# Drains behind conv bursts, later Gram matmuls, and narrower second-phase loads in a ConvNeXt-V2 block kernel

## The chip, the cores and the metric

The kernel runs on one core of one Trainium2 chip. The metric is the device time of a run in microseconds (us), best read as the median of several runs. Every run quoted here was in the fast state, with a granted TensorE clock of 0.988 to 0.998. Profiled executions are 1.7 to 1.9 us shorter by their span than by their time, so spans are compared with spans and times with times.

## The reference, cut to what matters

```python
# x: [1, 512, 512, 96] bf16
out = depthwise_conv3x3(x, dw)                 # zero padding
h = layernorm(out)                             # over the 96 channels
h = gelu(h @ w1)                               # 96 -> 384
gx = sqrt((h * h).sum(over all pixels) + 1e-6) # one number per expanded channel
nx = gx / (gx.mean() + 1e-6)
h = grn_gamma * (h * nx) + grn_beta + h
return x + h @ w2                              # 384 -> 96
```

The sum over all pixels splits the work in two. The first phase must have seen every pixel's `gelu` before the second can multiply by `w2`. There are 128 blocks of 4 image rows. `gelu` of a block is too big to keep for all of them, so the first phase writes the normalised input `yn` (and one of four column quarters of `g = gelu(...)`) to DRAM, and the second phase reads both back and recomputes the missing quarters.

Of the kernel before, what the change touches and what calls it, by code (L numbers as in the profile page):

```python
# [12 lines left out]
GR = 4  # L13
# [40 lines left out]
def kernel(  # L54
# [10 lines left out]
    nc = tc.nc  # L65
    f32 = mybir.dt.float32
    i32 = mybir.dt.int32
    bf16 = x.dtype
# [7 lines left out]
    NCH = E // 128  # L76
    NG = W // 128
    NBLK = H // GR
    BATCHES = batches_of(NBLK)

    QW = GR * 128
    NQ = GR * W // QW
    dram = ctx.enter_context(tc.tile_pool(name="dram", bufs=1, space=bass.MemoryType.DRAM))
    g_dram = dram.tile([NBLK, 128, NCH * QW], bf16, name="g_dram")
    yn_dram = dram.tile([NBLK, C, GR * W], bf16, name="yn_dram")
    r_dram = dram.tile([NBLK, GR, W], bf16, name="r_dram")

    def is_res(q):
        return q >= NBLK - RES
# [2 lines left out]
        return 3 if q % 3 and not is_res(q) else 2  # L92

    def kept_quads(q):
        return 2 if is_res(q) else 1

    def chans(i):
        return slice(i, 64, 2) if i < 2 else slice(64, 96)
# [1 line left out]
    PXP = GR * W // 128  # L100
# [9 lines left out]
        return yn_dram[q].rearrange("c (r w) -> c r w", r=GR)  # L110

    def yn_rows(q):
        return yn_dram[q:q + 2].rearrange("q c w -> (q c) w")[0:128]

    def yn_dst(q, r):
        return yn_dram[q].rearrange("(c i) (r w) -> r c i w", i=NI, r=GR)[r]
# [40 lines left out]
    p2 = ExitStack()  # L157
    SL = PXP + 2
    with ExitStack() as p1:
        pe, dve, act, pool, sp = (InOrder(tc, e) for e in (nc.tensor, nc.vector, nc.scalar, nc.gpsimd, nc.sync))  # L160
# [67 lines left out]
        for i in range(NXT):  # L228
            t = xtpool.tile([128, NI, SL * MB], bf16, name=f"xT{i}")
# [3 lines left out]
        GPS = max(d for d in range(1, cap + 1) if PXP % d == 0)  # L233
        NSUB = PXP // GPS

        def stage_load(n, sq, pq):
            q = ORDER[n]
            v = (ORDER[0] + n) % NYT
            r0 = q * GR
            if is_res(q):  # L240
                kept, ynt = res_g[q], ynts[q]
            else:
                kept = late.gl.tile([128, 1, NCH, QW], bf16, name="gl")
                (pq if q % 3 == 0 else sq).dma_start(  # L244
                    out=kept[:].rearrange("p t j w -> p (t j w)"), in_=g_dram[q])
                ynt = yn_ring[v]
                sq.dma_start(out=ynt[:].rearrange("p r w -> p (r w)"), in_=yn_rows(q))
            xr = late.xr.tile([128, PXP, C], bf16, name="xr")
            pq.dma_start(out=xr[:], in_=x[0, r0:r0 + GR].rearrange("r w c -> (r w) c").rearrange(  # L249
                "(p g) c -> p g c", g=PXP))  # L250
            grp[q] = dict(kept=kept, ynt=ynt, xr=xr)
# [21 lines left out]
        def stage_xb(q, pq, bias):  # L273
            if q is None:
                return
            xb = late.xb.tile([128, PXP, C], f32, name="xb")
            pq.tensor_tensor(out=xb[:], in0=grp[q]["xr"][:],  # L277
                                    in1=bias[:, None, :].to_broadcast([128, PXP, C]), op=ALU.add)
            grp[q]["xb"] = xb

        def stage_mm2(n, q):
            kept, made, xb = grp[q]["kept"], grp[q]["made"], grp[q]["xb"]
            nk = kept_quads(q)
            GQ = QW // 128
            o_sb = late.o.tile([128, PXP, C], bf16, name="o_sb")
            for sub in range(NSUB):
                O = late.psO.tile([128, GPS, C], f32, name="O")
                for gl_ in range(GPS):
                    gg = sub * GPS + gl_
                    for j in range(NCH):  # L290
                        t, c = gg // GQ, gg % GQ * 128
                        if t < nk:
                            lhsT = kept[:, t, j, c:c + 128]
                        else:
                            c += (t - nk) * QW
                            lhsT = made[:, j, c:c + 128]
                        pe.matmul(O[:, gl_, :], lhsT=lhsT, rhs=W2s[:, j, :],
                                   start=(j == 0), stop=(j == NCH - 1))
                dve.tensor_tensor(out=o_sb[:, sub * GPS:(sub + 1) * GPS, :], in0=O[:],
                                   in1=xb[:, sub * GPS:(sub + 1) * GPS, :], op=ALU.add)  # L300
                pace(n, sub)
            grp.pop(q)
            return o_sb

        def stage_out(q, o_sb):
            r0 = q * GR
            nc.sync.dma_start(  # L307
                out=out[0, r0:r0 + GR].rearrange("r w c -> (r w) c").rearrange("(p g) c -> p g c", g=PXP),
                in_=o_sb[:])
# [16 lines left out]

        def pace(n, sub):
            due = sum(1 for v in todo if v <= n + 1) if sub == NSUB - 1 else 0
            even = LEAD + (n * NSUB + sub + 1) * total / (NSUB * NBLK)
            advance(max(due, even), n + PRE)  # L330

        SG = psS.tile([128, 2 * NS + NCH * 128], f32, name="SG")
# [72 lines left out]
        def conv_taps(b, spare):  # L405
            if spare:
                Ua = psU.tile([128, 2, W], f32, name="U")
                Ub = psU.tile([128, 2, W], f32, name="U")
                Y = [Ua[:, 0, :], Ua[:, 1, :], Ub[:, 0, :]]
            else:  # L410
                Y3 = psY.tile([128, NI, W], f32, name="Y")
                Y = [Y3[:, i, :] for i in range(NI)]
            mms = []
            for n in range(3):
                mms.append([(h, j, (n + h) % NI, dx) for dx in (0, -1, 1) for j in range(GR) for h in range(2)])
            flat = [m for ms in mms for m in ms]
            first = {}
            last = {}
            for n, (h, j, i, dx) in enumerate(flat):
                first.setdefault((i, j), n)  # L420
                last[i, j] = n

            def burst(n):
                k = sum(len(ms) for ms in mms[:n])
                if n:
                    pe.drain()
                for h, j, i, dx in mms[n]:
                    src = b + shift(h, j)
                    o0, o1 = max(0, -dx), W - max(0, dx)
                    pe.matmul(  # L430
                        Y[i][32 * j:32 * j + 32, o0:o1],
                        lhsT=Wq[64 * h:64 * h + 64, i, dx + 1, j, :],
                        rhs=x_rows(src, 64 * h, 64 * h + 64, i, MB * (1 + dx) + o0, o1 - o0)
                        if 0 <= src < NBLK else zrow[64 * h:64 * h + 64, o0:o1],
                        start=first[i, j] == k,
                        stop=last[i, j] == k,
                    )
                    k += 1

            def evac():  # L440
                y = ypool.tile([128, NI, W], bf16, name="y_bf")
                if spare:
                    act.activation(out=y[:, 0:2, :], in_=Ua[:], func=ACTF.Identity)
                    act.activation(out=y[:, 2, :], in_=Ub[:, 0, :], func=ACTF.Identity)
                else:
                    act.activation(out=y[:], in_=Y3[:], func=ACTF.Identity)
                ybf[b] = y

            return [lambda n=n: burst(n) for n in range(3)], evac
# [158 lines left out]
        def mlp_units(b):  # L608
# [45 lines left out]
                        entry(j, 2, gms[b][:, j * QW:(j + 1) * QW])  # L654

            def store():
                sp.dma_start(out=g_dram[b], in_=gsh[:, 0].rearrange("p j w -> p (j w)"))

            return pair, rest, squares, squares_rest, store

# [57 lines left out]
        for s in range(last_slot + 1):  # L718
# [56 lines left out]
            else:  # L775
                b = mlp[0]
                pair, rest, squares, squares_rest, put_out = mlp_units(b)
                conv = lambda n: taps[n]() if taps else None
                conv(0)
                if not taps:  # L780
                    for b2 in get("gram"):
                        if b2 != b:
                            gram_mms(b2)
                pair(0)
                pair(1)
                squares(0)
                conv(1)
                spread_out()
# [31 lines left out]
            if s == last_slot - 3:  # L820
                pc.close()
                late.psO = p2.enter_context(tc.tile_pool(name="psO", side="right", bufs=2, space=bass.MemoryType.PSUM))
                late.xr = p2.enter_context(tc.tile_pool(name="xr", side="right", bufs=5))
                late.xb = p2.enter_context(tc.tile_pool(name="xb", side="right", bufs=3))
                late.gr = p2.enter_context(tc.tile_pool(name="gr", side="right", bufs=4))
                late.gl = p2.enter_context(tc.tile_pool(name="gld", side="right", bufs=6))
                late.o = p2.enter_context(tc.tile_pool(name="o", side="right", bufs=4))
            for n in {2: (0, 1, 2), 1: (3, 4)}.get(last_slot - s, ()):
                stage_load(n, sp, pool)
# [14 lines left out]
    with p2:  # L844
# [39 lines left out]
                                    op0=ALU.mult)  # L884
        dve2.tensor_copy(out=B2c[:], in_=B2bc_f[:])

        held = None
        for n, q in enumerate(ORDER):
            if n + PRE < NBLK:
                stage_load(n + PRE, nc.sync, nc.gpsimd)  # L890
            if n + 2 < NBLK:
                stage_xb(ORDER[n + 2], nc.gpsimd, B2c)
            o_sb = stage_mm2(n, q)
            if held:
                stage_out(*held)
            held = (q, o_sb)
        stage_out(*held)


# [28 lines left out]
```

## The kernel before: the parts that the change and the argument touch

The **first phase** runs in slots. One slot convolves block s and runs the MLP of an earlier block. TensorE makes the conv in three bursts of 24 small tiled matmuls (accumulating in PSUM tile `Y`), and between them the MLP matmuls into one of two PSUM buffers `U`. A drain (`pe.drain()`) is an instruction that makes TensorE wait between two groups of matmuls; what one costs here is measured in e1_drain. ScalarE turns each `U` into `gelu` (`gsh`, `gm`) and moves `Y` out (`y_bf`). Sums of squares come from VectorE (`bst`) and from small Gram matmuls of `gm` with itself (`SG`).

```python
def burst(n):                      # one third of the conv
    k = sum(len(ms) for ms in mms[:n])
    if n:
        pe.drain()                 # the next burst adds to a bank that the last one wrote
    for h, j, i, dx in mms[n]:
        pe.matmul(Y[i][...], lhsT=Wq[...], rhs=x_rows(...), ...)

# a slot with an MLP (cut)
conv(0)                            # taps[0], or nothing once the image is done
if not taps:
    for b2 in get("gram"):         # Gram matmuls of the previous block
        if b2 != b:
            gram_mms(b2)
pair(0); pair(1)                   # 2 x 2 matmuls into U, ScalarE: gsh
squares(0)
conv(1)
pair(2)
conv(2); evac()                    # ScalarE: y_bf
rest(0); stage_stats(...); rest(1) # ScalarE: gm
if taps:
    for b2 in get("gram"): ...
rest(2)
```

The **second phase** goes block by block. GpSimd adds the bias to the residual (`xb`), TensorE recomputes `U` and multiplies by `w2` into `O`, VectorE adds `xb` and writes `o_sb`.

```python
def stage_load(n, sq, pq):         # sq: SyncE, pq: GpSimd; called 5 blocks ahead
    kept = late.gl.tile([128, 1, NCH, QW], bf16, name="gl")
    (pq if q % 3 == 0 else sq).dma_start(out=kept..., in_=g_dram[q])     # 384 KB
    sq.dma_start(out=ynt[:]..., in_=yn_rows(q))                          # 512 KB
    pq.dma_start(out=xr[:], in_=x[...])                                  # 384 KB

def pace(n, sub):                  # how far the recompute may run ahead, in units of a third of a block
    due = ...
    even = LEAD + (n * NSUB + sub + 1) * total / (NSUB * NBLK)           # LEAD = 8
    advance(max(due, even), n + PRE)

for n, q in enumerate(ORDER):
    stage_load(n + PRE, nc.sync, nc.gpsimd)
    stage_xb(ORDER[n + 2], nc.gpsimd, B2c)   # xb, 3 buffers
    o_sb = stage_mm2(n, q)                   # O and o_sb (4 buffers), pace() after each of 4 parts
    if held: stage_out(*held)                # the block before goes out, 384 KB
    held = (q, o_sb)
stage_out(*held)
```

## Time and profile before

| | before |
|---|---|
| time, median of 3 runs | 1587.96 us (1584.48 to 1589.34) |
| profiled span | 1581.4 us |
| slots with conv, to 941 us | 7.49, 7.49, 7.64 us (median of each third slot, from the starts of `y_bf`) |
| 14 slots without conv, to 1041 us | 6.8 us, one of 9.4 |
| second phase, first to last start of `xb` behind the statistics | 521.8 us for 126 blocks |

Lines marked L32 belong to a helper that records every operation in program order, so one goes by the tiles' names. First the page's busy tenths, in 40 slices of the span: 9 is 90% or more.

```profile
PE   7889999999999999999999986689999999999998
ACT  3879999999999999999999997899999999999997
POOL 3559888989989898988989896349999999899997
DMA  5668787787777787787778666679999999999996
```

In the second phase (from slice 27) four resources look full. The Trainium skill (Trainium Kernel Development and Optimization, Performance Expectations) calls matmul busy time a bad metric for distance from the roofline; TensorE reads 97% busy in the window at the end of this section.

Next, the timeline of ScalarE over a slot with conv: start, duration of the group, engine, operation, tiles, count, and in brackets the idle time before it.

```profile
508.37 2.85 ACT L32 ACTIVATE gm<-U 128x1024 bf16<-128x1024 f32 x3
511.46 2.98 ACT L32 ACTIVATE gsh<-U 128x1024 bf16<-128x1024 f32 x3 [0.24 <-ACT gm L32]
514.53 1.45 ACT L32 ACTIVATE y_bf<-Y 128x1536 bf16<-128x1536 f32 x1
```

ScalarE stands 0.24 us before the first `gsh`. The 2.98 us of three `gsh` (2.85 when they follow each other without a gap) hold another short wait, before the third, and `y_bf` starts 0.09 us after the last `gsh` ended. The TensorE timeline of the same slot:

```profile
509.71 0.33 PE L32 MATMUL U<-w1p,ynT 128*128 128x384 bf16 x1
509.96 0.88 PE L32 MATMUL Y<-xT,Wq 64*32 64x512 bf16 x24
510.77 1.09 PE L32 MATMUL U<-ynT,w1p 128*128 128x512 bf16 x4
511.97 0.88 PE L32 MATMUL Y<-xT,Wq 64*32 64x512 bf16 x24
512.78 0.61 PE L32 MATMUL U<-ynT,w1p 128*128 128x512 bf16 x2
```

From the start of a burst to the next U matmul it is 0.81 us (510.77 - 509.96). From the four U matmuls to the second burst, which waits for the drain, it is 1.20.

ScalarE in slots without conv:

```profile
965.83 2.86 ACT L32 ACTIVATE gsh<-U 128x1024 bf16<-128x1024 f32 x3 [1.19 <-issue]
968.56 2.88 ACT L32 ACTIVATE gm<-U 128x1024 bf16<-128x1024 f32 x3
972.63 2.85 ACT L32 ACTIVATE gsh<-U 128x1024 bf16<-128x1024 f32 x3 [1.19 <-issue]
```

It stands 1.19 us in every 6.8: the Gram matmuls need the last `gm`, and `pair(0)` stands behind them on TensorE.

GpSimd in the second phase:

```profile
1267.02 0.55 POOL L249 DMA_DIRECT2D xr<-in_x_dram  x1 [0.30 <-POOL xb L277]
1267.59 3.15 POOL L277 TENSOR_TENSOR xb<-xr,B2c 128x1536 f32<-128x1536 bf16 x1
1271.03 0.55 POOL L249 DMA_DIRECT2D xr<-in_x_dram  x1 [0.30 <-POOL xb L277]
1271.58 0.54 POOL L244 DMA_DIRECT2D gl<-g_dram  x1
1272.13 3.14 POOL L277 TENSOR_TENSOR xb<-xr,B2c 128x1536 f32<-128x1536 bf16 x1
```

A block takes GpSimd 4.0 us, and 4.54 when it also issues a load of `g` (one in three): 4.18 on average. What VectorE waited for from 1150 to 1500 us (total us, times, longest):

```profile
DVE o_sb L32 <- PE O L32: 113.9, 201, 1.5
DVE o_sb L32 <- POOL xb L277: 47.3, 44, 1.7
DVE o_sb L32 <- DMA out_dram<-o_sb: 5.6, 4, 1.9
```

And one window of the second phase: stretch, its length, busy us of PE, PEld, DVE, ACT, POOL with counts, granted clock, share of the DMA engines, GB/s.

```profile
1400.00:1500.00 100.00, 97.14 (x1365) 69.95 (x1362) 50.96 (x97) 98.07 (x73) 92.40 (x56) 1.00 1.02 409
```

### The profile page before, as it was taken

Reading aid. Unit: us, or ns where it says so; the run is one execution under the profiler, and the core shown is the slowest. Engines: PE = TensorE matmul, PEld = TensorE weight load, DVE = VectorE, ACT = ScalarE, POOL = GpSimd, SP = SyncE. Lnnn points to the kernel's source line nnn. Section 1 sums busy time; section 2 is a strip of 40 time slices with the busy share of each in tenths; the row PEclk is TensorE's granted clock in tenths of the full one; section 3 lists DMA queues with packets and bytes.
Section 4 is the critical chain, followed back from the end, with each engine's and each line's share of the span. In section 5 each row is a group of like instructions: output and inputs, shape, how many; then the busy total and the mean of one; then the engine's idle time right before and its main releaser. Section 6 shows DMA issues by size and latency. Waiting matters only on the chain. (4 is left out here: it accounts for less than half of the span.)

```text
span 1581.4 us, 55730 instructions
## 1 busy us (share of the span) xinstructions
PE 1461.4 (92%) x23749; PEld 845.8 (53%) x23749; DVE 1129.2 (71%) x2027; ACT 1461.4 (92%) x1306; POOL 1316.3 (83%) x933
## 2 busy tenths in 40 slices
PE   7889999999999999999999986689999999999998
PEld 2434444444444444444444443357777676676766
DVE  6848978888888888888898877755555555555545
ACT  3879999999999999999999997899999999999997
POOL 3559888989989898988989896349999999899997
PEclk8999999999999999999999999999999999999999
DMA  5668787787777787787778666679999999999996
GB/s 146 180 186 264 226 260 212 237 258 227 232 235 246 218 261 222 227 246 239 216 235 254 196 193 200 202 253 412 412 412 412 409 410 408 405 409 408 409 408 259
DMA packets 186654, 444.45 MB, mean 281 GB/s; under 512 B 34054, under 2 KB 83302, under 8 KB 186406
## 3 DMA queue, kind: packets, MB, share of 16 engines
q1 hardware_dynamic: 171156, 373.10, 70.1%
q0 software_dynamic: 13888, 67.64, 10.9%
q8 instruction: 186, 3.05, 0.8%
q14 instruction: 62, 0.51, 0.1%
q10 hardware_dynamic: 1362, 0.15, 0.1%
HBM read 289.30 MB, written 150.72 MB: 278 GB/s over the span
## 5 line engine op out<-in xcount | busy, mean ns | idle before, releaser
L32 PE MATMUL U<-ynT,w1p 128*128 128x512 bf16 x2166 | 606.1, 381 | 17.5 <-ACT gsh L32 13.2
L32 DVE BATCH_NORM_STATS2 bst<-gsh 128x6 f32<-128x512 bf16 x756 | 468.5, 673 | 145.5 <-ACT gsh L32 145.5
L32 ACT ACTIVATE gr<-U 128x1536 bf16<-128x1536 f32 (+1 forms) x384 | 521.1, 1453 | 11.1 <-PE U L32 8.1
L32 POOL TENSOR_TENSOR yn<-y_bf,rbc 128x1536 bf16<-128x1536 bf16 x128 | 397.0, 3104 | 87.0 <-DMA rbc<-r_dram 39.8
L32 DVE TENSOR_TENSOR o_sb<-O,xb 128x384 bf16<-128x384 f32 x512 | 277.4, 556 | 251.2 <-PE O L32 181.2
L277 POOL TENSOR_TENSOR xb<-xr,B2c 128x1536 f32<-128x1536 bf16 x126 | 394.7, 3134 | 47.8 <-DVE B2c L32 44.8
L32 ACT ACTIVATE gsh<-U 128x1024 bf16<-128x1024 f32 x378 | 370.3, 1022 | 50.5 <-ACT gm L32 17.3
L32 ACT ACTIVATE gm<-U 128x1024 bf16<-128x1024 f32 x384 | 367.9, 1032 | 0.1
L32 PE MATMUL Y<-xT,Wq 64*32 64x511 bf16 (+1 forms) x8694 | 323.4, 389 | 35.0 <-DVE B2bc_f L32 3.7
L32 POOL TENSOR_TENSOR ysq<-y_bf 128x1536 bf16<-128x1536 bf16 x114 | 313.1, 2747 | 17.8 <-ACT y_bf L32 17.4
L32 PEld LDWEIGHTS <-w1p 128*128 128x128 bf16 x2166 | 168.1, 98 | 243.7 <-issue 161.0
L32 PEld LDWEIGHTS <-gr 128*128 128x128 bf16 x4584 | 236.3, 98 | 109.1 <-issue 26.4
L32 PE MATMUL O<-W2s,gr 128*128 128x96 bf16 x4584 | 256.8, 206 | 11.0 <-DVE o_sb L32 9.2
L32 PEld LDWEIGHTS <-Wq 64*32 64x32 bf16 x9216 | 105.9, 91 | 227.2 <-issue 188.9
L32 ACT ACTIVATE y_bf<-Y 128x1536 bf16<-128x1536 f32 x121 | 175.5, 1450 | 24.9 <-PE Y L32 17.8
L32 PE MATMUL U<-w1p,ynT 128*128 128x384 bf16 (+2 forms) x1032 | 161.4, 272 | 34.0 <-ACT gm L32 29.9
L32 DVE STREAM_TRANSPOSE xT<-xin 128x576 f32<-128x576 f32 (+1 forms) x256 | 181.4, 747 | 4.0 <-DMA xin<-in_x_dram 3.0
L32 DVE BATCH_NORM_STATS2 bst<-gm 128x6 f32<-128x512 bf16 x252 | 156.5, 676 | 1.5 <-ACT gm L32 1.5
L32 PE MATMUL SG<-gm 128*128 128x128 bf16 x2064 | 139.6, 220 | 11.1 <-ACT gm L32 8.5
L32 PEld LDWEIGHTS <-ynT 128*128 128x128 bf16 x1032 | 88.8, 97 | 90.4 <-issue 69.2
L32 PEld LDWEIGHTS <-gm 128*128 128x128 bf16 x2064 | 120.9, 98 | 23.8 <-ACT gm L32 13.7
L249 POOL DMA_DIRECT2D xr<-in_x_dram x123 | 68.1, 553 | 35.9 <-POOL xb L277 35.6
(103 smaller groups left out, 694.0 us busy)
## 6 DMA issues: line engine op xcount, KB each, us to landing
ynT<-yn_dram SPq DMA_DIRECT2D x126, 512.0 KB
xin<-in_x_dram SPq DMA_DIRECT2D x126, 432.0 KB
yn_dram<-yn SPq DMA_DIRECT2D x512, 96.0 KB
ynT<-yn_dram SPq DMA_DIRECT2D x128, 384.0 KB
xr<-in_x_dram POOLq DMA_DIRECT2D x128, 384.0 KB, 6.7
out_dram<-o_sb SPq DMA_DIRECT2D x128, 384.0 KB
g_dram<-gsh SPq DMA_DIRECT2D x126, 384.0 KB
gl<-g_dram SPq DMA_DIRECT2D x84, 384.0 KB
```

Source lines behind the costliest of these rows:

```text
L32: r = f(*a, **k)
L249: pq.dma_start(out=xr[:], in_=x[0, r0:r0 + GR].rearrange("r w c -> (r w) c").rearrange("(p g) c -> p g c", g=PXP))
L277: pq.tensor_tensor(out=xb[:], in0=grp[q]["xr"][:], in1=bias[:, None, :].to_broadcast([128, PXP, C]), op=ALU.add)
```

## The change

It puts the drain behind bursts 0 and 1 instead of ahead of bursts 1 and 2; puts the Gram matmuls behind `pair(0)` and `pair(1)` in slots without conv; loads only those columns of `yn` that are expanded again; keeps two quarters of `g` in DRAM for every fourth block, so less is recomputed; changes the pacing of the recompute; and sends the last block out in four parts. The core of the diff, with cuts:

```diff
 def kept_quads(q):
-    return 2 if is_res(q) else 1
+    return 2 if is_res(q) or q % 4 == 2 else 1
 def yn_rows(q):
-    return yn_dram[q:q + 2].rearrange("q c w -> (q c) w")[0:128]
+    k = kept_quads(q) * 128
+    return yn_dram[q:q + 2].rearrange("q c (r w) -> (q c) r w", r=GR)[0:128, :, k:]
 ... (loads and stores of g with nk quarters; a second pool gl2; gl from 6 to 5 buffers)
 def pace(n, sub):
-    even = LEAD + (n * NSUB + sub + 1) * total / (NSUB * NBLK)
+    even = LEAD + (n * NSUB + sub + 1) * (total + 2 - LEAD) / (NSUB * NBLK)
 def burst(n):
-    if n:
-        pe.drain()
     for h, j, i, dx in mms[n]: ...
+    if n < 2:
+        pe.drain()
 conv(0)
+pair(0)
+pair(1)
 if not taps:
     for b2 in get("gram"): ...
-pair(0)
-pair(1)
 ... (the last block's output in four DMAs, issued as its parts are made)
```

## The prediction

> **What bounds the kernel now.** Three stretches, from the busy-time windows and timelines.
> 1. 0 to 941 us, conv+MLP slots: ScalarE starts y_bf every 7.5 us (7.64 each third). Neither ScalarE nor TensorE is full. They pass two U buffers back and forth; per slot ScalarE stands about 0.28 us before the first gsh and 0.2 before the third, TensorE about 0.35 before the last gm group.
> 2. 941 to 1041 us, 14 slots without conv: 6.8 us each (one 9.4), ScalarE idle 1.19 us before the first gsh of every slot, because the previous block's Gram matmuls wait for the last gm and stand ahead of pair(0).
> 3. 1049 to 1581 us, second phase. TensorE and ScalarE read 100% busy and DMA 1.03 of its engines (412 GB/s), but the chain of waits and the POOL timeline name GpSimd: xb 3.13 + 0.30 wait + xr issue 0.55 = 4.0 us a block, plus 0.54 for gl in every third: 4.18 mean. 126 blocks from 1049.4 end at 1574.4, then 7 us of last block. TensorE needs about 4.0, ScalarE 4.03, DMA about 4.1: all just under GpSimd.
>
> **What the change does.**
> - Drains. A drain between U and conv matmuls makes their start-to-start 0.485 us against about 0.25 without. A natural conv-to-U turn is 0.316; conv-drain-conv in spare slots is 0.50. So moving two drains costs about 2 x 0.19 and saves 2 x 0.23. The Trainium skill (TensorE: Matmul & The Clock Gate, Step-by-step) says a stream normally overlaps the array's drain with the next fill; an explicit drain gives that up on either side, and conv-to-U already half pays it. The first drain lands ahead of pair(0) (a ScalarE wait grows), the second relieves pair(2). An estimate of the ping-pong from these durations, which gives 7.44/7.44/7.61 before, gives about 7.4/7.4/7.47 after: 0.07 us x 112 slots = -8 us (0 to -15).
> - Gram later: removes the 1.19 in slots with 12 Gram matmuls, about half of it with 24, which now stand ahead of pair(2); also hides the single 2.6 us wait on the SG memset. -13 us (-8 to -16).
> - Second phase: every fourth block loses 3 U matmuls and a third of its gelu (0.65 us TensorE, 1.3 us ScalarE); bytes per block fall from 1664 to 1600 KB on average. GpSimd's work is unchanged, so the pace stays 4.18: no gain. DMA: packets cost 46/121/159 ns for 1024/3072/4096 bytes, about 8 ns fixed plus 37 per KB (the Trainium skill, DMA: Bandwidth & Descriptors, "Why small descriptors are slow", has a fixed overhead per packet; the fit agrees). 512 runs of 768 B: 18.7 us of engine time against 20.4 for 128 of 4096; per four blocks the larger g eats this: +1%, an estimate. DMA then sits at the GpSimd pace; expected loss +4 us (0 to +15).
> - Last output in parts: -0.5 us. Drain savings and fewer matmuls cannot shorten GpSimd's 126 blocks; the second phase just starts earlier.
>
> **Predicted** 1571 us, 8 in 10 between 1557 and 1585; faster by over 2% 0.12, within 2% 0.84, slower 0.04.
>
> **What would show it.** y_bf spacing falling to about 7.4, its first-gsh wait growing to 0.45; conv-free slots near 5.8 to 6.4 us; xb of GpSimd still every 4.0/4.0/4.54 us and the second phase still about 525 us from first xb to last, with more idle on ScalarE and TensorE; DVE waiting for xb more often.
>
> **What would make it wrong.** (a) The drain behind conv dearer than 0.23: first stretch neutral or slower. (b) 768/512 B runs dearer than the fit: xb or U waits on yn loads, second phase paced by DMA (+15 or more). (c) GpSimd's 0.30 wait or xb being lengthened by ScalarE/DMA traffic, so relief shortens it: faster by over 2%.

## The result, and the profile after

The ratio is the mean time of one kernel's fast runs over that of the other's fast runs of the same rounds, so it is not quite the ratio of the medians quoted.

| | before | after |
|---|---|---|
| time, median of 4 | 1586.4 us | 1565.45 us (1562.6 to 1569.31) |
| ratio | | 0.9868 (0.9837 to 0.9899), within 2% |
| slots with conv | 7.49, 7.49, 7.64 us | 7.45, 7.45, 7.63 us |
| last `y_bf` to last first `gsh` (14 slots without conv) | 96.5 us | 79.5 us |
| first to last `xb` | 521.8 us | 512.4 us |
| last `xb` to the end of the span | 10.1 us | 18.4 us |

The last two rows cancel nearly: 531.9 against 530.8 us. So the gain lies in the first phase, and almost all of it in the slots without conv.

ScalarE and TensorE in slots with conv, after:

```profile
507.19 2.85 ACT L32 ACTIVATE gm<-U 128x1024 bf16<-128x1024 f32 x3
510.46 2.92 ACT L32 ACTIVATE gsh<-U 128x1024 bf16<-128x1024 f32 x3 [0.42 <-ACT gm L32]
513.29 1.45 ACT L32 ACTIVATE y_bf<-Y 128x1536 bf16<-128x1536 f32 x1
```

```profile
508.26 0.60 PE L32 MATMUL U<-w1p,ynT 128*128 128x256 bf16 x4 [0.33 <-ACT gm L32]
508.79 0.87 PE L32 MATMUL Y<-xT,Wq 64*32 64x512 bf16 x24
509.77 1.03 PE L32 MATMUL U<-ynT,w1p 128*128 128x512 bf16 x4
510.73 0.87 PE L32 MATMUL Y<-xT,Wq 64*32 64x512 bf16 x24
```

Burst to U grew from 0.81 to 0.98 us, and the four U matmuls to the next burst fell from 1.20 to 0.96. The wait before the first `gsh` grew to 0.42, the one inside the three fell (2.98 to 2.92 us), and `y_bf` no longer waits (13.29, ahead of the modelled end of `gsh` at 13.38). Over the 107 slots between 100 and 930 us in which three `gsh` stand between `gm` and `y_bf`, the medians from start to start are: last `gm` to first `gsh` 1.30 us before and 1.48 after, second to third `gsh` 1.02 and 0.98, third `gsh` to `y_bf` 1.09 and 0.92. The loss of 0.18 at the first and the gain of 0.21 at the other two leave about 0.03 us a slot.

ScalarE in slots without conv, after (the first holds 24 Gram matmuls, the next 12):

```profile
962.28 1.97 ACT L32 ACTIVATE gsh<-U 128x1024 bf16<-128x1024 f32 x2
964.87 1.02 ACT L32 ACTIVATE gsh<-U 128x1024 bf16<-128x1024 f32 x1 [0.62 <-PE U L32]
965.79 2.85 ACT L32 ACTIVATE gm<-U 128x1024 bf16<-128x1024 f32 x3
968.50 2.94 ACT L32 ACTIVATE gsh<-U 128x1024 bf16<-128x1024 f32 x3
```

The 1.19 us is gone. With 24 Gram matmuls half of it comes back ahead of the third `gsh`, since they now stand before `pair(2)`. Slots take 5.55 or 6.22 us.

GpSimd in the second phase, after:

```profile
1149.52 0.56 POOL L251 DMA_DIRECT2D xr<-in_x_dram  x1 [0.30 <-POOL xb L279]
1150.10 3.13 POOL L279 TENSOR_TENSOR xb<-xr,B2c 128x1536 f32<-128x1536 bf16 x1
1153.16 0.56 POOL L246 DMA_DIRECT2D gl<-g_dram  x1
1153.72 0.54 POOL L251 DMA_DIRECT2D xr<-in_x_dram  x1
1154.27 3.15 POOL L279 TENSOR_TENSOR xb<-xr,B2c 128x1536 f32<-128x1536 bf16 x1
```

Here the scheduler happened to place `gl` ahead of `xr`, and the 0.30 us wait is gone from that block: 4.17 us instead of 4.54. In the built program `gl` stands first in 28 of 40 cases; before, `xr` stood first in all 41.

VectorE's waits and one window, after:

```profile
DVE o_sb L32 <- POOL xb L279: 81.6, 65, 3.6
DVE o_sb L32 <- PE O L32: 70.6, 155, 1.3
```

```profile
1400.00:1500.00 100.00, 95.66 (x1358) 69.31 (x1357) 51.93 (x98) 91.40 (x73) 94.15 (x56) 1.00 1.04 400
```

TensorE and ScalarE were relieved and stand idle a little more; VectorE waits for `xb` more. Then the end of the kernel, on TensorE:

```profile
1543.48 0.41 PE L32 MATMUL O<-W2s,gr 128*128 128x96 bf16 x2
1545.01 0.60 PE L32 MATMUL O<-W2s,gr 128*128 128x96 bf16 x10 [1.12 <-ACT gr L32]
...
1550.54 0.60 PE L32 MATMUL O<-W2s,gr 128*128 128x96 bf16 x10 [1.13 <-ACT gr L32]
```

TensorE stands 1.12 us in each of these blocks for a `gelu` that was asked for only just before. Block by block, from the end of each block's last `o_sb` (us per block, means of 16 blocks, the last of 15):

```
before                     4.03 4.03 4.15 4.19 4.32 4.17 4.20 3.90
after                      3.83 4.00 4.13 4.08 4.35 4.03 4.06 4.51
```

What the second phase gains on the way it gives back in the last 16 blocks. (The 4.32 and 4.35 hold one stop of 2 to 4 us that both kernels have; it was not looked into.)

### The profile page after: what moved, and what is told of

It reads as the page before. It is cut to its first block, busy times and chain, and to the rows that moved or that the text cites. A ratio compares the mean times of both kernels' runs of the same rounds, so it can differ in the third digit from the quotient of the medians.

```text
span 1561.5 us, 55590 instructions
## 1 busy us (share of the span) xinstructions
PE 1436.4 (92%) x23656; PEld 835.3 (53%) x23656; DVE 1127.8 (72%) x2027; ACT 1413.7 (91%) x1306; POOL 1315.6 (84%) x933
## 5 line engine op out<-in xcount | busy, mean ns | idle before, releaser
L32 PE MATMUL U<-ynT,w1p 128*128 128x512 bf16 x2073 | 583.9, 381 | 44.0 <-ACT gm L32 8.0
L32 ACT ACTIVATE gr<-U 128x1536 bf16<-128x1536 f32 (+1 forms) x384 | 487.7, 1345 | 47.5 <-PE U L32 45.0
L32 PEld LDWEIGHTS <-w1p 128*128 128x128 bf16 x2073 | 159.4, 98 | 267.8 <-issue 177.9
L32 PEld LDWEIGHTS <-gr 128*128 128x128 bf16 x4212 | 211.0, 98 | 95.9 <-issue 27.7
L32 PE MATMUL O<-W2s,gr 128*128 128x96 bf16 x4212 | 231.8, 206 | 25.0 <-DVE o_sb L32 15.4
L32 PEld LDWEIGHTS <-Wq 64*32 64x32 bf16 x9216 | 102.1, 90 | 188.2 <-issue 147.6
L32 PE MATMUL SG<-gm 128*128 128x128 bf16 x2064 | 136.3, 219 | 0.5 <-ACT gm L32 0.3
L32 PEld LDWEIGHTS <-gl 128*128 128x128 bf16 x1884 | 95.1, 98 | 28.0 <-issue 0.6
```

Of the source, the lines that this page charges most:

```text
L32: r = f(*a, **k)
```

## The experiments

All kernels gave correct results. Each ran on one chip beside the kernel before, whose median was 1585 to 1586 us. "Span of xb" is from the first to the last start of `xb` behind the statistics.

| run | time, us | ratio (95%) | span of xb, us |
|---|---|---|---|
| e1_drain | 1581.86 | 0.9977 (0.9958 to 0.9995) | 521.8 |
| e2_gram | 1568.3 | 0.9888 (0.987 to 0.9907) | 523.3 |
| e3_lead | 1562.89 | 0.9857 (0.9838 to 0.9877) | 518.6 |
| e4_gl_sp | 1587.28 | 1.0006 (0.9989 to 1.0024) | 522.0 |
| e7_cols | 1585.08 | 1.0008 (0.998 to 1.0036) | 522.0 |
| e9_cols_sp | 1570.2 | 0.9899 (0.988 to 0.9918) | 504.4 |
| e6_gl_pool | 1630.42 | 1.0282 (1.0253 to 1.031) | 566.5 |
| e5_lead_sp | 1557.84 | 0.9823 (0.9805 to 0.984) | 510.9 |
| e11_pace_sp | 1562.93 | 0.986 (0.9842 to 0.9878) | 509.5 |
| e12_glfirst | 1570.66 | 0.991 (0.9891 to 0.9929) | 504.4 |
| e13_best | 1550.8 | 0.9786 (0.9762 to 0.981) | 504.4 |

### e1_drain: the drains alone

```diff
 # kernel before
-    if n:
-        pe.drain()
     for h, j, i, dx in mms[n]: ...
+    if n < 2:
+        pe.drain()
```

> The kernel before with the two drains moved behind the bursts, nothing else. Theory (measured turns): a drain costs 0.18 us on either side of a burst, so TensorE's total is unchanged and only the place of the wait moves; slots go from 7.49 to about 7.45 us, 112 slots, total -2 to -5 us. Rival (the prediction's sum, 0.25 without a drain): slots 7.4, total -8 us or more. ScalarE's wait before the first gsh of a slot grows by 0.1 to 0.2 us under both.

Measured: ratio 0.9977, about -3.6 us. Slots 7.46, 7.46, 7.63. The instruction records give the start-to-start times of the turns. With 512 columns in the last matmul, U to conv takes 0.309 us without a drain and 0.485 with one; conv to U takes 0.316 without and 0.499 with one. So a drain costs 0.18 us on either side of a burst. (A turn without a drain is not free either: two U matmuls of 512 columns follow each other in 0.216.) Moving a drain changes whom it delays, and hardly how much TensorE works. The first theory holds: the interval allows -0.8 to -6.7 us and leaves out the rival's -8. ScalarE's starts moved as in the changed kernel (1.49, 0.98 and 0.92 us in the three places named above).

### e2_gram: the Gram matmuls alone

```diff
 # kernel before
 conv(0)
+pair(0); pair(1)
 if not taps: ... gram_mms(b2)
-pair(0); pair(1)
```

> The kernel before with the Gram matmuls after pair(0) and pair(1) in slots without conv, nothing else. Theory: the 14 conv-free slots fall from 6.8 to 5.55 (12 Gram matmuls) and 6.2 us (24), and the single 9.4 us slot loses its extra 2.6; total -15 to -18 us, second phase unchanged (first to last xb 522 us). Rival: part of the gain in the changed kernel's last slots comes from the drains or from the phase-2 loads, so this alone gives under 12 us.

Measured: ratio 0.9888, -17.8 us. Slots without conv 5.55 and 6.22 us, the one of 9.38 became 6.22, and the slot in which the conv ends fell from 8.65 to 7.28. The second phase did not change (523.3). This one move is worth 85% of the whole gain of the change (17.8 of 20.9 us, both by the ratios).

### e4_gl_sp: GpSimd freed of its g loads

```diff
 # kernel before
-(pq if q % 3 == 0 else sq).dma_start(
+sq.dma_start(
     out=kept..., in_=g_dram[q])
```

> The kernel before with every g load issued by SyncE (GpSimd issued a third of them). Bytes, TensorE and ScalarE work are unchanged. Theory (GpSimd paces the second phase): its block falls from 4.18 to 4.0, after which ScalarE (4.03) and DMA (about 4.1) bind; first to last xb 522 to 507-514 us, total -7 to -15 us. Rival (DMA or TensorE and ScalarE pace it): no change, within 2 us.

Measured: nothing, ratio 1.0006. The theory that GpSimd alone paces the second phase fell here. GpSimd did get faster by itself: VectorE no longer waited for `xb` at all, but for something else.

```profile
DVE o_sb L32 <- PE O L32: 110.9, 204, 1.4
DVE o_sb L32 <- DMA out_dram<-o_sb: 54.1, 57, 2.6
```

Before, the wait for output buffers was 5.6 us, now it is 54.1: they come free too late, that is, the DMA transfers are behind. The pace stayed near 4.18. The next theory: two bounds of equal length stand side by side, GpSimd's own work and the DMA engines, so that relief of one shows nothing. This asks for relief of each and of both.

### e7_cols and e9_cols_sp: DMA relieved alone, and both relieved

```diff
 # kernel before; e7_cols: these two edits, e9_cols_sp: also the edit of e4_gl_sp
 def yn_rows(q):
-    return yn_dram[q:q + 2].rearrange("q c w -> (q c) w")[0:128]
+    k = kept_quads(q) * 128
+    return yn_dram[q:q + 2].rearrange("q c (r w) -> (q c) r w", r=GR)[0:128, :, k:]
-sq.dma_start(out=ynt[:]..., in_=yn_rows(q))
+sq.dma_start(out=ynt[:, :, kept_quads(q) * 128:], in_=yn_rows(q))
```

> The kernel before with only the expanded yn columns loaded (1536 KB a block instead of 1664), nothing else. Two-bounds theory: DMA is relieved but GpSimd still takes 4.18, so first to last xb stays 520-523 us and the total within 3 us of before. Rival (DMA alone paces, as the run with g on SyncE may be read): pace 3.9 to 4.1, total -8 us or more.

> The kernel before with both: only the expanded yn columns loaded and every g load on SyncE. Two-bounds theory: each alone gives nothing, both together give a pace of 4.03 to 4.08 (ScalarE 4.03 is next): first to last xb 505-512 us, total -9 to -17 us. Rival (a third thing paces, for instance TensorE and ScalarE at their real rate): no change, within 3 us.

Measured: 522.0 us for the columns alone, 522.0 for GpSimd alone, 504.4 for both. Nothing, nothing, and -15 us together (ratios 1.0008, 1.0006, 0.9899). VectorE's waits with the columns alone:

```profile
DVE o_sb L32 <- POOL xb L278: 82.3, 71, 4.0
```

The wait for GpSimd is still there, and for output buffers there is none left. With both:

```profile
DVE o_sb L32 <- PE O L32: 155.5, 261, 0.7
```

```profile
1400.00:1500.00 100.00, 100.00 (x1419) 73.63 (x1417) 55.31 (x100) 100.00 (x76) 88.96 (x50) 1.00 1.04 393
```

Only TensorE's ordinary wait is left, and the pace is 4.03 us in all but the last group of blocks. The chain that ended last, from 1150 to 1500 us, says the same without going by busy shares (shares of this stretch; "issue" is time in which the engine waited for nothing that the profile shows). In this order: before, e4_gl_sp, e7_cols, e9_cols_sp:

```profile
by line: POOL xb L277 39.4%; DMA out_dram<-o_sb 21.5%; PE O L32 13.4%; PE U L32 11.1%; POOL xr L249 5.7%; issue 4.7%; POOL gl L244 2.8%; DVE o_sb L32 1.9%; POOLq L277 0.1%; SPq L244 0.1%; POOLq L244 0.1%; DVEq L32 0.0%; SPq L307 0.0%
by line: DMA out_dram<-o_sb 30.1%; PE O L32 26.1%; PE U L32 23.0%; DMA ynT<-yn_dram 19.3%; DMA gl<-g_dram 3.2%; DVE o_sb L32 2.1%; issue 0.5%; DVEq L32 0.1%; SPq L307 0.0%; SPq L247 0.0%
by line: POOL xb L278 30.5%; PE O L32 29.8%; PE U L32 27.8%; POOL gl L245 3.4%; issue 2.9%; POOL xr L250 2.8%; DVE o_sb L32 2.8%; POOLq L278 0.1%; POOLq L245 0.0%
by line: PE O L32 50.7%; PE U L32 49.3%
```

Before, the chain runs over GpSimd and over DMA in turn. With g on SyncE GpSimd is gone from it, with the columns DMA is gone, and with both only TensorE is left. The number of DMAs on the SyncE queue is no rival here: e9_cols_sp issues as many on it for each block as e4_gl_sp does, and only the `yn` load differs (384 KB in place of 512).

The 4.03 us belong to TensorE and ScalarE together. `gelu` starts 1.343 us apart on average (3 x 1.343 = 4.03), but TensorE's 9 U and 48 O matmuls, at the 0.216 and 0.0425 us in which they follow each other, come to 3.98 us by themselves, so this run does not part the two. The window shows why busy shares hid all this: PE, ACT and the DMA share read 100, 100 and 1.04 where TensorE and ScalarE are the bound, and 97, 98 and 1.02 before, where they were not and a block took 4% longer. The GB/s (393 against 409) tell that DMA has less to move.

### e6_gl_pool: more on GpSimd

```diff
 # kernel before
-(pq if q % 3 == 0 else sq).dma_start(
+pq.dma_start(
     out=kept..., in_=g_dram[q])
```

> The kernel before with every g load issued by GpSimd (a third before). If GpSimd's own work paces the second phase whenever it is the longest, a block takes 4.54 us: first to last xb about 566 us, total +40 to +47 us. If DMA alone paces and GpSimd only looks busy, within 5 us of before.

Measured (two runs): 566.5 us, 4.533 us a block, ratio 1.0282, +45 us. GpSimd's work is a bound in its own right. DMA alone, or TensorE and ScalarE alone, do not explain this.

### e3_lead, e5_lead_sp and e11_pace_sp: the pacing, with and without GpSimd in the way

```diff
 # changed kernel; e3_lead: the first edit, e11_pace_sp: the second, e5_lead_sp: both
-    even = LEAD + (n * NSUB + sub + 1) * (total + 2 - LEAD) / (NSUB * NBLK)
+    even = LEAD + (n * NSUB + sub + 1) * total / (NSUB * NBLK)
-(pq if q % 3 == 0 else sq).dma_start(
+sq.dma_start(
```

> The changed kernel with the old pacing of the recompute (lead of 8 units kept to the end). Theory: the new formula lets the lead shrink from 8 units to 2, so that in the last 16 blocks TensorE waits for gelu just made; the last 16 blocks return from 4.28 and 4.79 us to 4.1 or less, total 6 to 10 us below the changed kernel, about 1557. Rival: the last blocks are slow because the small yn loads arrive late (DMA); then the pace stays and the time is within 2 us of the changed kernel.

> The changed kernel with the old pacing of the recompute and every g load on SyncE, so that GpSimd only issues xr (4.0 us a block). If two bounds stand side by side in the second phase (GpSimd 4.18, DMA 4.18 before) and DMA follows the bytes (1600 against 1664 KB), the pace falls to about 4.03: first to last xb 505 to 512 us, about 1552. If DMA follows the packet times (+1% against before), it stays DMA-bound at 4.18 to 4.23 and the time is that of the changed kernel with the old pacing, 1563 or more.

> The changed kernel with every g load on SyncE but with its own new pacing (the partner of the run with the old pacing and g on SyncE, 1557.8). If the shrinking lead costs time by itself, the last 16 blocks are again near 4.5 us (3.83 with the old pacing) and the whole is 6 to 11 us slower, about 1566. If the lead is harmless once GpSimd is relieved: within 2 us of 1557.8.

Measured: 1562.89 with the old pacing, 1562.93 with g on SyncE, 1557.84 with both; the changed kernel had 1565.45. The paces (us a block, by 16 blocks):

```
after                      3.83 4.00 4.13 4.08 4.35 4.03 4.06 4.51
e3_lead                    3.91 4.01 4.19 4.15 4.32 4.19 4.13 3.87
e11_pace_sp                3.83 4.01 4.15 4.05 4.13 4.02 4.10 4.51
e5_lead_sp                 3.91 3.98 4.19 4.12 4.14 4.15 4.09 3.83
```

The old pacing mends the end in both pairs (4.51 to 3.87 and 3.83; 0.65 us x 15 blocks is 10 us). That is not its net worth: up to the 113th block the kernels with the new pacing are ahead, by 6.6 us in the first pair and 4.3 in the second, so that over the second phase the new pacing costs 2.5 and 5.0 us. TensorE's waits in the last 70 us of the run with the new pacing and g on SyncE,

```profile
PE O L32 <- ACT gr L32: 7.9, 12, 1.1
```

are the same as in the changed kernel, and in the run with the old pacing and g on SyncE this wait does not occur. So the small loads of `yn` are not the cause of the slow end; the lead is, which the new formula lets shrink from 8 units to 2. Both gains came out smaller than expected: 2.6 us in the first pair, where 6 to 10 were expected, and 5.1 in the second, just under the 6 that were expected. By the ratios to the kernel before, the first gain is not clear of noise (0.9857 and 0.9868, with overlapping intervals) and the second is. Why the new pacing is ahead until the end stays open. In the first pair the scheduler put `gl` first in only 9 of 40 cases with the old pacing, instead of 28, and 19 waits of 0.30 us would be 5.7 of the 6.6 us. But with g on SyncE, where that order can't matter, the new pacing is ahead too (4.02 against 4.15 in the sixth group).

The two expectations for DMA in the run with both edits (pace 4.03 if it follows the bytes, 4.18 to 4.23 if it follows packet times) were both missed: it is 4.09 to 4.19 in the middle, with VectorE waiting 46.7 us for output buffers, so DMA-bound and in between. (The span of `xb`, 510.9 us, does lie in the 505 to 512 that went with the first; the 1552 us that went with it do not fit.)

### e12_glfirst: GpSimd's loads in program order

```diff
 # kernel before with the two edits of e7_cols, and
-    stage_load(n + PRE, nc.sync, nc.gpsimd)
+    stage_load(n + PRE, nc.sync, pool)          # pool: the wrapper that keeps program order
-    stage_xb(ORDER[n + 2], nc.gpsimd, B2c)
+    stage_xb(ORDER[n + 2], pool, B2c)
```

> The kernel before with the expanded columns only (which alone gave nothing: 522 us from first to last xb) and GpSimd's loads kept in program order, so that g is issued ahead of xr in every third block. Theory: issuing g first hides the 0.30 us wait ahead of xr under it; that block takes 4.17 instead of 4.54, the mean 4.06, first to last xb about 507 us, total -13 to -16 us. Rival (the order of two issues does not matter): 522 us, no change.

Measured: ratio 0.991, 504.4 us, as with g on SyncE. It went beyond the expectation: the 0.30 us wait ahead of `xr` vanished from all blocks and not only from those with `gl`, so the 4.03 us of TensorE and ScalarE became the bound. The run shows that about 0.3 us of GpSimd's block was avoidable without moving any work, and that the order in which the scheduler set GpSimd's instructions was worth some 15 us once DMA was relieved. It doesn't isolate the order of `gl` and `xr`, because it removed the other waits too. What the wait is for stays open.

### e13_best: without the second kept quarter

```diff
 # changed kernel with both edits of e5_lead_sp, and
-    return 2 if is_res(q) or q % 4 == 2 else 1
+    return 2 if is_res(q) else 1
```

> The changed kernel with the old pacing, every g load on SyncE, and no second quarter kept (so drains, Gram, columns only). Theory: the two kept quarters add DMA time (512 B runs and 384 KB more g) and DMA paces at 4.1; without them ScalarE paces at 4.03: first to last xb 504 instead of 511 us, about 1551. Rival (the kept quarters help by relieving ScalarE): slower than 1557.8.

Measured: 1550.8 us, ratio 0.9786 (0.9762 to 0.981), faster than both kernels: about 34 us below before and 13 below the changed kernel by the ratios. Whether it is more than 2% below before is just not settled by the interval. Span of xb 504.4 against 510.9 with the second quarter kept. So that part of the change costs time here: it relieves ScalarE and TensorE, and DMA, which it loads more (1600 against 1536 KB a block), was the tighter bound: VectorE's wait of 46.7 us for output buffers is gone in this run. By the ratios the two intervals just touch (0.9805 and 0.981).

## Why the prediction was right or wrong, point by point

The total (1571 forecast, 1565.45 measured, range 1557 to 1585) and the verdict "within 2%" held. Its terms were less good, and that the total came this close is partly luck: the drains were booked 4.4 us too high and the Gram move 4.8 too low.

- **Drains, forecast -8 us, measured -3.6.** The mechanism was right in its first half: the wait before the first `gsh` grew, by 0.18 us. Of the relief, which the prediction put at pair(2), only 0.04 us came at the third `gsh`; 0.17 came at `y_bf`, which waits for the third burst and which the prediction doesn't name. The mis-sized term is "about 0.25 [us] without" a drain. That number came from turns whose last U matmul has 384 columns; with 512 columns, as ahead of the drained bursts, it is 0.309. So moving a drain saves 0.18 and not 0.23, which is what it costs on the other side. The skill's account of overlapping drain and fill (TensorE: Matmul & The Clock Gate, Step-by-step) agrees with this trace where matmuls of one shape follow each other (216 ns start to start for 512 columns); an explicit drain adds 0.18 us at either place, which fits an overlap that is lost.
- **Gram later, forecast -13, measured -17.8.** Right in mechanism, and the halves were right too (1.25 us off a slot with 12, 0.58 off one with 24). The sum was booked too low: the named pieces, 9 x 1.19, 4 x 0.6 and 2.6, already make 15.7, and the slot in which the conv ends, which lost another 1.4, was not in it.
- **Second phase, "GpSimd's work is unchanged, so the pace stays 4.18: no gain".** The outcome (531.9 to 530.8 us from the first `xb` to the end) matches, for the wrong reason. Three steps failed. First, GpSimd was not the one bound: DMA, put at "about 4.1", stood at the same 4.18, shown by e4, e7 and e9. Second, GpSimd's time did change, since the scheduler reordered its two issues: the 0.30 us wait ahead of `xr` stood in all 121 blocks looked at before and in 91 of 119 after. Point (c) of the prediction had named a shorter wait as a risk, though from less traffic and not from another order. Third, the new pacing formula, which the prediction doesn't mention, cost about 10 us in the last 16 blocks. That ate what the second phase had gained up to there, of which 4 to 7 us came with the same formula.
- **DMA, packets of 768 and 512 bytes.** The fit gave 36.6 ns for 768 bytes (18.7 us for 512 runs); the trace after shows medians of 36 ns for 768 and 27 for 512 bytes. The fixed overhead per packet that the Trainium skill describes (DMA: Bandwidth & Descriptors, Why small descriptors are slow) agrees in kind: about 8 ns of each packet here by the fit. (The page counts its overhead in cycles, which no run here can be compared with.) The forecast loss of 4 us did not show in the total; with GpSimd relieved and the old pacing the second kept quarter did cost time (span of `xb` 510.9 us with it in e5_lead_sp, 504.4 without in e13_best).
- **Last output in parts, forecast -0.5.** The time from the last `o_sb` to the end fell from 3.4 to 2.9 us in the changed kernel, but it is 3.1 to 4.0 us in the other four kernels that have this edit, so the gain isn't shown.

## What to carry to other kernels

When several resources read full at once, a test that relieves only one of them proves nothing if it shows no gain: relieve each alone and both together, as e4, e7 and e9 do. Count the instructions that an engine issues for others (0.55 us for a DMA on GpSimd) as part of its work, and look at the order that a scheduler chose for them after every edit. When one formula sets how far one stage runs ahead of another, look at the last blocks separately, because there a lost lead costs most.

## What the Trainium skill lacked or had wrong

- TensorE: Matmul & The Clock Gate has no cost for an explicit drain instruction. Here it costs 0.18 us, whether it stands between U and conv (0.309 to 0.485 us) or between conv and U (0.316 to 0.499).
- DMA: Bandwidth & Descriptors, Issuing engines are not separate DMA queues, calls the sequencer time saved by issuing from several engines "usually small relative to the DMA itself". That is so (0.55 us against 7 us to landing), but on an engine that also computes it is no small thing: one more issue per block in two blocks of three cost 45 us in 1585 (e6), and one fewer in one of three gained 15 once DMA was relieved (e9 against e7).
- No page tells of the wait of 0.30 us that GpSimd showed ahead of a DMA issue behind its own arithmetic, nor that it can vanish with another order of instructions (e12).
- DMA: Bandwidth & Descriptors, Specifications, gives 512 bytes as the least transfer for line rate. Here a packet of 512 bytes took 27 ns (after) and one of 4096 took 159 (before), so a byte costs 36% more at 512 (27/512 against 159/4096).
- The same table's limit of about 358 GB/s for HBM per core is a stack's rate split between two cores, and the page says so only further down. This one-core program moved 409 GB/s in the window shown of the second phase before, so who reads the row alone sets the bound too low.
